# Moving a bias load and reordering the first steps of a fused attention and dense kernel on one core

## The chip, the cores and the metric

The kernel runs on one core of one Trainium2 chip. The metric is the device time of one execution in microseconds (us). A profiled execution also gives a trace; its span runs from the first to the last instruction. In the profile PE is TensorE, PEld its weight loads, DVE VectorE, ACT ScalarE, POOL GpSimd and SP the engine that issues most DMAs; ACTq and SPq are the queues on which ACT and SP issue.

## The reference

Input x is 2048 x 512 in bf16. It is normalised once, and two branches use the result:

```
xn = layernorm(x)
A: q, k, v = xn @ wqkv, in 32 heads of 16
   pq, pk = q @ w_phi, k @ w_phi            (16 x 16 per head)
   phi(p) = [softmax(p), softmax(-p)]
   kv = phi_k^T v;  z = sum of phi_k
   A = ((phi_q kv) / (phi_q z + 1e-6)) @ wo
B: h = xn @ w1 + b1                          (1792 hidden units)
   B = (h * tanh(softplus(h))) @ w2          (Mish)
out = x + A + B
```

## The kernel before

The 2048 tokens are 16 tiles of 128, in four groups of four. w_phi is folded into the key and query weights: `wT`, the key (later the query) part of wqkv, is loaded turned by a transposing DMA (line 143); `Wbd` holds w_phi as a block-diagonal matrix (line 524); the fold (line 156) multiplies the two, and its result is copied to `wkp` (line 165).

The order of the work is written by hand: the scheduler is off, and one string, `STEPS`, lists 433 steps, which line 623 issues one after the other. Each engine takes its own instructions in that order and waits only on data and buffers. `@n` behind a step is the PSUM bank it takes, one of six; a step that takes a bank waits until the bank's last reader is done. `v` or `a` behind a copy says whether DVE or ACT makes it. The steps that matter here:

- `LS i`, `RS i`, `AZ i`, `TP i`, `TC i`: for the four tiles of group 0, statistics (170, 172), inverse root on POOL (176, 177), normalisation (181), turning on PE (560), copy of the turned tile to `xnT` (565). `LN g` and `AP g k` do the same for a later group, turned by DMA (186).
- `WB`: Wbd. `F0 kt`, `FD kt`: fold and copy for the keys; `WT`, `F`, `FC` the same for the queries.
- `PB`: the bias, loaded as 14 x 128, is turned on PE (533); `CB` copies it to `b1f` (605), which every Mish reads.
- `LP`: the first two tiles' key logits (209). `L s i`, `LC`: logits of a tile (194) and their copy (252); `WL` the same in a wide bank. `V t`, `VC t`: values (194) and copy (218). `H u`, `M u`: one 128-unit piece of the hidden layer for four tiles (228) and its Mish (239).
- `E`, `X`, `S`, `R`, `N`: extremes, exponentials (288), sums (305), inversion and scaling (340) of the softmaxes; `A` accumulates kv (387); `KV` masks it; `W`, `Q`, `G`, `C` do the queries (366, 418, 433, 455).
- `O t`, `P t`, `Y t`: second layer (463), projection by wo (470), addition of x and store (477, 478). `OH`, `PH`, `YH` are the last tile in two parts.
- `DX g`, `DW i`: loads of x groups 2 and 3 and of w2 and wo, on SP.

Before the first step the kernel issues the loads of lines 483 to 493 and, on PE, `WARM` matmuls on a constant (513), which compute nothing that is used:

```
nc.sync.dma_start(x_sb[:, 0, :], x_v[:, 0, :])
wT_of = {0: load_turned(D)}
...
nc.scalar.dma_start(wsrc[:], wphi_v)
nc.scalar.dma_start(x_sb[:, 1, :], x_v[:, 1, :])
nc.scalar.dma_start(b1b[:], b1_v[:, :])
nc.sync.dma_start(x_sb[:, 2:4, :], x_v[:, 2:4, :])
nc.sync.dma_start(wv[:], wqkv_v[:, :, 2 * D : 3 * D])
nc.sync.dma_start(w1_sb[:, :, 0 : 7 * P], w1_v[:, :, 0 : 7 * P])
nc.sync.dma_start(x_sb[:, 4:8, :], x_v[:, 4:8, :])
nc.sync.dma_start(w1_sb[:, :, 7 * P : F], w1_v[:, :, 7 * P : F])
```

The line numbers in the text are those of the kernel before; in the changed kernel they are one lower in most places.

Of the kernel before, what the change touches and what calls it, by code (L numbers as in the profile page):

```python
# [19 lines left out]

WARM = 12
STEPS = """
LS 0; RS 0; DX 2; LS 1; WB; RS 1; AZ 0; TP 0 @0; F0 0 @1; F0 1 @2; AZ 1; FD 0 v; TP 1 @3; TC 1 v; LS
2; PB @4; RS 2; TC 0 a; LS 3; RS 3; FD 1 a; AZ 2; F0 2 @5; F0 3 @0; FD 2 a; FD 3 a; LP i @1,2; KM;
DX 3; AZ 3; V 0 @3; LC 0 0 a; TP 2 @5; V 1 @0; TC 2 a; TP 3 @1; VC 0 a; LC 0 1 v; TC 3 v; CB; L 0 2
@5; L 0 3 @2; LC 0 3 a; LN 1; H 0 @3; H 1 @1; H 2 @4; M 0; LC 0 2 a; H 3 @2; M 1; M 2; M 3; VC 1 a;
E 0 0; H 4 @3; H 5 @5; AP 1 0; H 6 @1; H 7 @4; M 4; H 8 @2; M 5; H 9 @0; M 6; M 7; H 10 @3; M 8; M
9; M 10; AP 1 1; H 11 @5; E 0 1; V 4 @1; X 0 1; WL 1; LN 2; V 6 @4; VC 4 a; X 0 0; L 1 0 @2; L 1 3  # L30
@0; LC 1 0 a; V 5 @3; LN 3; VC 5 a; H 12 @1; WL 2; H 13 @2; VC 6 a; S 0 0; LC 1 3 a; M 11; V 3 @3; M
12; M 13; H 14 @4; H 15 @0; H 16 @5; H 17 @1; VC 3 a; M 14; H 18 @2; M 15; M 16; M 17; LC 1 2 a; H
19 @3; AP 2 0; AP 2 1; AP 3 0; L 2 0 @4; LC 2 0 a; L 2 1 @0; LC 2 1 a; V 2 @5; S 0 1; L 2 2 @1; M
18; LC 1 1 a; M 19; H 20 @4; LC 2 2 a; AP 3 1; H 21 @0; WT; H 22 @2; M 20; VC 2 a; R 0 1 v; L 2 3
@3; H 23 @1; R 0 0 v; N 0 1; M 21; N 0 0; H 24 @4; M 22; LC 2 3 a; F 0 @5; F 1 @0; E 1 0; E 1 1; M
23; M 24; F 2 @2; E 2 0; E 2 1; FC 0 a; H 25 @3; H 26 @1; FC 1 a; H 27 @4; M 25; M 26; L 3 2 @5; FC
2 a; M 27; V 7 @0; L 3 3 @3; V 11 @1; F 3 @2; L 3 0 @4; LC 3 0 v; LC 3 2 a; L 3 1 @5; A 0 0; X 1 0;
X 1 1; A 0 1; LC 3 3 a; FC 3 v; S 1 0; V 8 @4; LC 3 1 a; VC 7 a; L 4 0 @2; E 3 0; VC 8 a; LC 4 0 a;
L 4 1 @3; LC 4 1 a; L 4 3 @5; VC 11 a; L 4 2 @0; X 2 0; V 9 @4; L 5 0 @2; H 28 @3; H 29 @1; VC 9 a;
LC 4 2 v; M 28; M 29; H 30 @0; H 31 @4; H 32 @3; M 30; H 33 @1; H 34 @0; M 31; M 32; M 33; M 34; H  # L40
35 @4; M 35; H 36 @3; M 36; S 1 1; LC 4 3 a; R 1 0 v; E 3 1; LC 5 0 a; N 1 0; R 1 1 v; H 37 @1; H 38
@0; H 39 @4; H 40 @3; H 41 @5; H 42 @2; S 2 0; A 1 0; M 37; N 1 1; M 38; M 39; M 40; A 1 1; M 41; M
42; X 3 0; L 6 3 @1; L 5 2 @0; V 10 @4; VC 10 a; L 5 1 @3; LC 5 2 a; L 6 0 @5; E 4 0; E 4 1; X 2 1;
S 3 0; V 15 @2; VC 15 a; V 13 @4; VC 13 a; LC 6 0 a; R 2 0 a; S 2 1; DW 3; R 3 0 a; X 3 1; L 6 1 @0;
LC 5 1 a; DW 2; N 3 0; N 2 0; L 5 3 @2; O 0 @4; S 3 1; V 12 @5; V 14 @3; LC 6 1 a; LC 5 3 a; O 1 @0;
L 6 2 @2; R 2 1 a; N 2 1; VC 14 a; LC 6 3 a; VC 12 v; R 3 1 a; N 3 1; X 4 0; A 2 0; S 4 0; LC 6 2 a;
A 2 1; A 3 0; W 4 0 v; X 4 1; H 43 @3; M 43; A 3 1; H 44 @1; H 45 @5; M 44; H 46 @2; M 45; H 47 @3;
M 46; M 47; H 48 @1; KV; H 49 @5; H 50 @2; Q 0 0; M 48; M 49; G 0 0; M 50; H 51 @3; H 52 @1; H 53
@5; S 4 1; W 4 1 v; M 51; M 52; H 54 @2; H 55 @3; Q 0 1; M 53; E 5 0; E 5 1; M 54; E 6 0; L 7 0 @1;
M 55; G 0 1; C 0 a; X 5 0; LC 7 0 a; L 7 1 @5; X 5 1; O 2 @2; O 3 @3; LC 7 1 a; L 7 2 @1; LC 7 2 a;  # L50
S 5 0; Q 1 0; L 7 3 @5; G 1 0; E 6 1; W 5 0 a; P 0; P 1; Y 0; Q 1 1; O 4 @1; G 1 1; LC 7 3 a; O 5
@4; S 5 1; Q 2 0; O 6 @5; C 1 a; P 2; G 2 0; W 5 1 v; Y 1; Q 2 1; P 3; O 7 @0; E 7 0; X 6 0; S 6 0;
G 2 1; Q 3 0; C 2 a; G 3 0; Y 2; Y 3; X 6 1; O 8 @2; Q 3 1; W 6 0 v; E 7 1; S 6 1; P 4; P 5; G 3 1;
C 3 a; Q 4 0; X 7 0; Y 4; W 6 1 v; X 7 1; S 7 0; O 9 @3; O 10 @1; G 4 0; Q 4 1; P 6; P 7; G 4 1; Y
5; Y 6; C 4 a; Q 5 0; W 7 0 a; G 5 0; O 11 @4; Q 5 1; Y 7; O 12 @5; S 7 1; G 5 1; C 5 a; Q 6 0; G 6
0; O 13 @0; Q 6 1; G 6 1; W 7 1 v; P 8; P 9; Q 7 0; C 6 a; G 7 0; P 10; P 11; Y 8; Q 7 1; G 7 1; O
14 @2; Y 9; Y 10; C 7 a; P 12; P 13; OH 0 @3; PH 0; Y 11; P 14; OH 1 @1; PH 1; Y 12; Y 13; YH 0; Y
14; YH 1
"""


# [1 line left out]
def kernel(  # L63
# [12 lines left out]
    nc = tc.nc  # L76
    P = 128
    S, D, NH, DH, F = 2048, 512, 32, 16, 1792
# [15 lines left out]
    b1_v = B_b1.rearrange("(f p) -> f p", p=P)  # L94
# [21 lines left out]
    b1b = wts.tile([FT, P], BF16, name="b1b")  # L116
# [29 lines left out]
    def bank(b, name, dtype=FP32):  # L146

        return ps.tile([P, 512], dtype, name=name, tag=f"bank{b}")
# [336 lines left out]
    with nc.allow_non_contiguous_dma(reason="tiny w_phi load"):  # L485
        nc.scalar.dma_start(wsrc[:], wphi_v)
    nc.scalar.dma_start(x_sb[:, 1, :], x_v[:, 1, :])
    nc.scalar.dma_start(b1b[:], b1_v[:, :])
    nc.sync.dma_start(x_sb[:, 2:4, :], x_v[:, 2:4, :])
    nc.sync.dma_start(wv[:], wqkv_v[:, :, 2 * D : 3 * D])  # L490
    nc.sync.dma_start(w1_sb[:, :, 0 : 7 * P], w1_v[:, :, 0 : 7 * P])
    nc.sync.dma_start(x_sb[:, 4:8, :], x_v[:, 4:8, :])
    nc.sync.dma_start(w1_sb[:, :, 7 * P : F], w1_v[:, :, 7 * P : F])

# [16 lines left out]
    warm = bank(5, "warm")  # L511
    for _ in range(WARM):
        nc.tensor.matmul(
# [142 lines left out]
```

## Time and profile before

| | us |
|---|---|
| median of 3 runs (lowest, highest) | 173.84 (173.68, 174.01) |
| the profiled execution, its own time | 174.0 |
| its span | 172.3 |
| ACT busy on Mish, 56 times | 37.2 |
| DVE busy on sums, 16 times | 36.4 |
| DVE idle for x from memory, 3 times | 4.3 |
| wv from issue to landing | 4.5 |

Busy time is what an engine spent in its instructions; matmuls overlap one another, so a busy PE does not say how closely they follow. For that the chain of work that ended last is read: it goes back from the last instruction, at each step to what released it or to the instruction ahead of it on its engine, and lists pieces as start, length and what. In the timeline a line is start, length, engine, source line, operation, output<-input and count, with the idle time ahead of it and its cause in brackets. In an answer on one source line the three durations are the least, the median and the greatest.

### The profile page before, as it was taken

The page shows a single profiled execution, that of the slowest core. Times are in us where ns is not written, and L with a number is a line of the kernel's source. Part 1 is how long each engine was busy: PE and PEld are TensorE (multiplying, and loading weights), DVE is VectorE, ACT ScalarE, POOL GpSimd, SP SyncE. Part 2 cuts the span into 40 slices and gives each one's busy share as a digit, 9 for nine tenths or more (in the row PEclk, how much of TensorE's full clock was granted, in tenths as well). Part 3 has the DMA queues.
Part 4 walks back from the last instruction along what each step waited for, and adds up shares of the span by engine and source line. Part 5 has one row for each costly group of instructions (what it writes and reads, how often), then busy time and mean ns, then how long its engine had stood idle before and what let it go on. Part 6 is the DMA issues. An engine that isn't in the chain of part 4 may idle for free.

```text
span 172.3 us, 2713 instructions
## 1 busy us (share of the span) xinstructions
PE 168.7 (98%) x1039; PEld 82.4 (48%) x1039; DVE 143.2 (83%) x221; ACT 119.5 (69%) x192; POOL 9.4 (5%) x26
## 2 busy tenths in 40 slices
PE   8999999999999999999999999999999999999993
PEld 2554444444545444454446544444444545445452
DVE  2878998999997999979999999799988996844433
ACT  2446889979899998989999988974063883414200
POOL 4332205000000000000000000000000000000000
PEclk9999999999999999999999999999999999999999
DMA  5999350199930000000000363023974749885641
GB/s 98 269 377 365 82 98 0 37 189 207 366 120 0 0 4 0 0 0 0 4 0 0 64 118 66 12 51 67 150 152 93 150 95 144 172 168 100 173 134 61
DMA packets 44953, 18.02 MB, mean 105 GB/s; under 512 B 37004, under 2 KB 44940, under 8 KB 44940
## 3 DMA queue, kind: packets, MB, share of 16 engines
q1 hardware_dynamic: 44096, 17.60, 44.5%
q10 hardware_dynamic: 844, 0.25, 0.6%
q8 instruction: 8, 0.13, 0.3%
q14 instruction: 5, 0.04, 0.1%
HBM read 6.84 MB, written 2.10 MB: 52 GB/s over the span
## 4 chain that ended last, share of the span: by engine, by line
PE 95%; DMA 3%; SPq 0%; DVE 0%; issue 0%
PE po L463 28%; PE ph L228 28%; PE pl L194 14%; PE po L470 8%; PE pv L194 8%; DMA wT<-in_A_wqkv_dram 3%; PE pnd L418 2%; PE pkv L387 2%; PE pfold L156 1%; PE pwide L194 1%; PE pl L209 1%; PE ptr L560 0%; SPq L483 0%; DVE x_sb L477 0%; PE pb L533 0%
## 5 line engine op out<-in xcount | busy, mean ns | idle before, releaser
L463 PE MATMUL po<-w_sb,acts 128*128 128x512 bf16 (+2 forms) x238 | 50.7, 366 | 0.0
L228 PE MATMUL ph<-xnT,w_sb 128*128 128x512 bf16 x224 | 50.1, 379 | 0.0
L239 ACT ACTIVATE acts<-ph,b1f 128x512 bf16<-128x512 f32 x56 | 37.2, 694 | 4.6 <-PE ph L228 4.4
L305 DVE TENSOR_REDUCE s<-e 128x128 f32<-128x2048 bf16 x16 | 36.4, 2279 | 2.5 <-ACT e L288 2.5
L228 PEld LDWEIGHTS <-w_sb 128*128 128x128 bf16 x224 | 21.7, 98 | 25.5
L463 PEld LDWEIGHTS <-acts 128*128 128x128 bf16 x238 | 22.3, 98 | 24.1
L288 ACT ACTIVATE e<-e 128x2048 bf16<-128x2048 bf16 x16 | 30.3, 1908 | 0.0
L194 PEld LDWEIGHTS <-xnT 128*128 128x128 bf16 x184 | 17.6, 98 | 20.1 <-DMA wv<-in_A_wqkv_dram 0.2
L252 ACT CAST p_sb<-pl 128x512 bf16<-128x512 f32 x27 | 15.4, 587 | 5.5 <-PE pl L194 4.7
L433 ACT COPY ds<-pnd 128x32 f32<-128x32 f32 x16 | 2.9, 183 | 23.5 <-PE pnd L418 23.5
L194 PE MATMUL pv<-wv,xnT 128*128 128x512 bf16 x64 | 16.1, 379 | 0.0
L477 DVE TENSOR_TENSOR x_sb<-po,x_sb 128x512 bf16<-128x512 f32 (+2 forms) x17 | 10.9, 654 | 5.7 <-PE po L470 5.7
L470 PE MATMUL po<-wqk,xnT 128*128 128x512 bf16 (+2 forms) x68 | 15.5, 366 | 0.0
L194 PE MATMUL pl<-wqk,xnT 128*128 128x512 bf16 x64 | 15.3, 379 | 0.0
L170 DVE BATCH_NORM_STATS2 stats<-x_sb 128x6 f32<-128x512 bf16 x16 | 10.1, 679 | 4.3 <-DMA x_sb<-in_A_x_dram 4.3
L263 DVE TENSOR_TENSOR m<-m 128x512 bf16<-128x512 bf16 (+1 forms) x32 | 11.5, 358 | 1.1
L194 PE MATMUL pl<-wkp,xnT 128*128 128x512 bf16 x48 | 11.7, 379 | 0.0
L263 DVE TENSOR_TENSOR m<-p_sb 128x1024 bf16<-128x1024 bf16 x16 | 10.9, 682 | 0.2 <-ACT p_sb L252 0.2
L272 DVE TENSOR_TENSOR e<-p_sb,m 128x2048 bf16<-128x2048 bf16 x8 | 9.8, 1226 | 1.4 <-PE pkv L387 1.1
L272 DVE TENSOR_TENSOR e<-m,p_sb 128x2048 bf16<-128x2048 bf16 x8 | 9.8, 1225 | 0.3
L340 DVE TENSOR_TENSOR e<-e,r 128x2048 bf16<-128x2048 bf16 x8 | 9.6, 1215 | 0.0
L138 ACT ACT_TABLE_LOAD x7 | 9.0, 1283 | 0.1
(62 smaller groups left out, 131.4 us busy)
## 6 DMA issues: line engine op xcount, KB each, us to landing
out_dram<-x_sb SPq DMA_DIRECT2D x15, 128.0 KB, 2.0
w_sb<-in_B_w_dram SPq DMA_DIRECT2D x2, 896.0 KB, 7.8
x_sb<-in_A_x_dram SPq DMA_DIRECT2D x3, 512.0 KB, 10.0
w_sb<-in_B_w_dram SPq DMA_DIRECT2D x2, 640.0 KB, 8.8
wv<-in_A_wqkv_dram SPq DMA_DIRECT2D x1, 512.0 KB, 4.5
wqk<-in_A_wo_dram SPq DMA_DIRECT2D x1, 512.0 KB, 4.6
w_sb<-in_B_w_dram SPq DMA_DIRECT2D x1, 512.0 KB, 9.6
x_sb<-in_A_x_dram SPq DMA_DIRECT2D x1, 256.0 KB, 3.2
```

The costliest lines, as they stand in the source:

```text
L170: nc.vector.bn_stats(stats[:, i, :], xs[:, i, :])
L194: nc.tensor.matmul(pp, lhsT=xnT[:, t, kt, :], rhs=w[:, kt, :], start=(kt == 0), stop=(kt == KT - 1),)
L228: nc.tensor.matmul(ph_of[u][:], lhsT=w1_sb[:, kt, f * P : (f + 1) * P], rhs=xnT[:, g * TPG : (g + 1) * TPG, kt, :], start=(kt == 0), stop= ...
L239: nc.scalar.activation(acts[:, f, g * 512 : (g + 1) * 512], ph_of.pop(u)[:], ACT.Mish, bias=b1f[:, f : f + 1])
L252: copy(p_of[s][:, i, :], pl_of.pop((s, i)))
L263: nc.vector.tensor_tensor(out=m[:], in0=src[:, :, 0:half], in1=src[:, :, half : 2 * half], op=op)
L272: nc.vector.tensor_tensor(out=e_of[s][:].rearrange("p t j l c -> p (t j) l c")[:, :, pl, :].rearrange("p t (c e o) -> p t c e o", e=8, o=2 ...
L288: nc.scalar.activation(v, v, ACT.Exp)
L305: nc.vector.reduce_sum(t[:], pair(s, k).rearrange("p t j l (c e) -> p (t j l c) e", e=16), axis=AX.X)
L463: nc.tensor.matmul(po_of[t, c.stop][:, c], lhsT=acts[:, f, t * P : (t + 1) * P], rhs=w2_sb[:, f, c], start=(f == 0), stop=False,)
L470: nc.tensor.matmul(po_of[t, c.stop][:, c], lhsT=oT_of[t // 2][:, t % 2 * 4 + j, :], rhs=wo_sb[:, j, c], start=False, stop=(j == 3),)
L477: nc.vector.tensor_tensor(out=y, in0=po_of.pop((t, c.stop))[:, c], in1=y, op=ALU.add)
```

## The change

- The bias is loaded on SP's queue behind the first half of w1, no longer on ACT's queue behind x's second tile.
- Eleven warm-up matmuls in place of twelve.
- The whole step list has a new order. In the head `AZ 0` and `TP 0` come ahead of `WB`; `PB` moves from among the folds to behind `L 0 3`; `H 0` comes ahead of `L 0 3`; `CB` comes behind `LN 1` on DVE; `LN 2` follows at once, ahead of `E 0 0`. Further on, steps of all kinds change places and banks, and some copies change engine: `VC` on ACT 15 to 11, `LC` on ACT 29 to 30, `R` on ACT 4 to 6, `C` on ACT 8 to 7, the rest of each on DVE.

The steps themselves and their functions are unchanged. The diff, with the step list cut after its head:

```
-WARM = 12
+WARM = 11
 STEPS = """
-LS 0; RS 0; DX 2; LS 1; WB; RS 1; AZ 0; TP 0 @0; F0 0 @1; F0 1 @2; AZ 1; FD 0 v; TP 1 @3; TC 1 v; LS
-2; PB @4; RS 2; TC 0 a; LS 3; RS 3; FD 1 a; AZ 2; F0 2 @5; F0 3 @0; FD 2 a; FD 3 a; LP i @1,2; KM;
-DX 3; AZ 3; V 0 @3; LC 0 0 a; TP 2 @5; V 1 @0; TC 2 a; TP 3 @1; VC 0 a; LC 0 1 v; TC 3 v; CB; L 0 2
-@5; L 0 3 @2; LC 0 3 a; LN 1; H 0 @3; H 1 @1; H 2 @4; M 0; LC 0 2 a; H 3 @2; M 1; M 2; M 3; VC 1 a;
-E 0 0; H 4 @3; H 5 @5; AP 1 0; H 6 @1; H 7 @4; M 4; H 8 @2; M 5; H 9 @0; M 6; M 7; H 10 @3; M 8; M
...
+LS 0; RS 0; LS 1; AZ 0; TP 0 @0; TC 0 a; WB; RS 1; F0 0 @1; F0 1 @2; AZ 1; FD 1 a; TP 1 @3; FD 0 v;
+F0 2 @4; F0 3 @5; TC 1 v; FD 2 a; FD 3 a; LP i @0,1; LC 0 0 a; DX 2; LS 2; LC 0 1 a; RS 2; LS 3; DX
+3; V 0 @2; RS 3; AZ 2; TP 2 @3; TC 2 a; V 1 @4; AZ 3; KM; TP 3 @5; L 0 2 @0; TC 3 v; LC 0 2 a; H 0
+@1; L 0 3 @3; VC 1 a; PB @5; LC 0 3 a; H 1 @0; H 2 @4; H 3 @3; LN 1; CB; LN 2; AP 1 0; AP 1 1; M 0;
+E 0 0; M 1; AP 2 0; E 0 1; M 2; M 3; LN 3; H 4 @1; M 4; V 3 @0; VC 3 a; VC 0 a; H 5 @5; H 6 @4; M 5;
...
+LC 3 1 a; V 5 @2; L 4 0 @1; E 2 1; VC 6 v; V 2 @5; L 4 3 @3; VC 2 a; LC 4 0 a; X 1 1; N 0 0; V 9 @4;
...
 """
@@
-    nc.scalar.dma_start(b1b[:], b1_v[:, :])
     nc.sync.dma_start(x_sb[:, 2:4, :], x_v[:, 2:4, :])
     nc.sync.dma_start(wv[:], wqkv_v[:, :, 2 * D : 3 * D])
     nc.sync.dma_start(w1_sb[:, :, 0 : 7 * P], w1_v[:, :, 0 : 7 * P])
+    nc.sync.dma_start(b1b[:], b1_v[:, :])
     nc.sync.dma_start(x_sb[:, 4:8, :], x_v[:, 4:8, :])
     nc.sync.dma_start(w1_sb[:, :, 7 * P : F], w1_v[:, :, 7 * P : F])
```

More of the change, by code (lines that the diff above doesn't have):

```diff
@@ L30 @@
[L30 to L58, printed above, removed]
+LS 0; RS 0; LS 1; AZ 0; TP 0 @0; TC 0 a; WB; RS 1; F0 0 @1; F0 1 @2; AZ 1; FD 1 a; TP 1 @3; FD 0 v;
+F0 2 @4; F0 3 @5; TC 1 v; FD 2 a; FD 3 a; LP i @0,1; LC 0 0 a; DX 2; LS 2; LC 0 1 a; RS 2; LS 3; DX
@@ new lines @@
+3; V 0 @2; RS 3; AZ 2; TP 2 @3; TC 2 a; V 1 @4; AZ 3; KM; TP 3 @5; L 0 2 @0; TC 3 v; LC 0 2 a; H 0
+@1; L 0 3 @3; VC 1 a; PB @5; LC 0 3 a; H 1 @0; H 2 @4; H 3 @3; LN 1; CB; LN 2; AP 1 0; AP 1 1; M 0;
+E 0 0; M 1; AP 2 0; E 0 1; M 2; M 3; LN 3; H 4 @1; M 4; V 3 @0; VC 3 a; VC 0 a; H 5 @5; H 6 @4; M 5;
+M 6; H 7 @3; M 7; H 8 @1; H 9 @0; M 8; H 10 @2; H 11 @5; H 12 @4; M 9; M 10; M 11; H 13 @3; WL 1; H
+14 @1; H 15 @0; L 2 0 @2; M 12; H 16 @5; M 13; X 0 0; LC 2 0 a; AP 2 1; X 0 1; L 1 0 @4; LC 1 0 v; S
@@ new lines @@
+0 0; L 1 3 @3; LC 1 3 a; H 17 @2; M 14; H 18 @4; V 4 @3; WL 2; M 15; M 16; M 17; M 18; AP 3 0; AP 3
+1; L 2 1 @1; H 19 @0; LC 1 2 a; M 19; H 20 @5; L 2 2 @2; LC 1 1 a; M 20; L 2 3 @4; H 21 @0; LC 2 3
+a; M 21; LC 2 2 a; H 22 @5; H 23 @4; H 24 @0; M 22; M 23; WT; F 0 @2; LC 2 1 a; FC 0 a; VC 4 v; H 25
+@3; R 0 0 v; H 26 @5; M 24; S 0 1; H 27 @4; F 1 @1; E 1 0; M 25; M 26; E 1 1; F 2 @2; F 3 @0; M 27;
+FC 3 a; FC 1 a; E 2 0; R 0 1 a; V 6 @3; V 7 @5; VC 7 a; X 1 0; L 3 0 @4; LC 3 0 a; L 3 1 @0; FC 2 v;
@@ new lines @@
+LC 3 1 a; V 5 @2; L 4 0 @1; E 2 1; VC 6 v; V 2 @5; L 4 3 @3; VC 2 a; LC 4 0 a; X 1 1; N 0 0; V 9 @4;
+S 1 0; VC 5 v; V 10 @0; L 4 2 @5; R 1 0 a; N 0 1; A 0 0; VC 9 v; V 8 @1; VC 8 v; LC 4 3 a; X 2 1; L
+3 3 @2; LC 3 3 v; X 2 0; S 1 1; L 3 2 @3; N 1 0; L 4 1 @4; LC 4 1 a; A 0 1; V 11 @1; VC 11 a; S 2 0;
+R 2 0 v; R 1 1 a; VC 10 a; LC 4 2 a; H 28 @2; H 29 @4; H 30 @1; N 1 1; LC 3 2 a; E 3 0; M 28; S 2 1;
+A 1 0; E 3 1; H 31 @0; H 32 @5; H 33 @3; H 34 @2; M 29; M 30; M 31; M 32; M 33; H 35 @4; H 36 @1; H
@@ new lines @@
+37 @0; H 38 @5; H 39 @3; M 34; M 35; N 2 0; DW 3; M 36; M 37; M 38; M 39; H 40 @2; H 41 @4; H 42 @1;
+M 40; M 41; H 43 @0; M 42; M 43; H 44 @5; M 44; H 45 @3; L 5 2 @2; A 1 1; A 2 0; L 5 3 @4; L 5 0 @1;
+H 46 @0; M 45; L 5 1 @5; X 3 1; LC 5 0 a; LC 5 3 a; E 4 0; E 4 1; LC 5 1 a; S 3 1; V 14 @3; V 12 @1;
+X 3 0; DW 2; VC 12 a; V 15 @4; S 3 0; O 0 @5; X 4 0; VC 14 a; V 13 @1; LC 5 2 a; L 6 0 @3; VC 15 a;
+L 6 2 @2; R 3 0 a; R 2 1 a; O 1 @4; S 4 0; R 3 1 a; LC 6 0 a; LC 6 2 a; VC 13 a; N 3 0; N 2 1; L 6 3
@@ new lines @@
+@3; H 47 @2; H 48 @1; N 3 1; A 2 1; W 4 0 v; A 3 0; A 3 1; E 5 0; X 4 1; KV; M 46; E 5 1; LC 6 3 a;
+M 47; M 48; H 49 @0; M 49; H 50 @3; H 51 @2; M 50; M 51; L 6 1 @1; S 4 1; H 52 @0; Q 0 0; G 0 0; M
+52; H 53 @3; LC 6 1 a; M 53; H 54 @2; Q 0 1; G 0 1; H 55 @0; M 54; L 7 0 @1; L 7 3 @3; E 6 0; M 55;
+W 4 1 v; L 7 2 @2; LC 7 0 a; O 2 @0; C 0 a; LC 7 3 a; X 5 0; O 3 @1; L 7 1 @3; LC 7 2 a; Q 1 0; X 5
+1; G 1 0; E 6 1; S 5 0; W 5 0 v; LC 7 1 a; O 4 @2; Q 1 1; G 1 1; P 0; S 5 1; C 1 a; O 5 @3; Y 0; X 6
@@ new lines @@
+0; Q 2 0; P 1; W 5 1 v; E 7 0; G 2 0; Y 1; O 6 @5; S 6 0; Q 2 1; P 2; P 3; Y 2; G 2 1; C 2 a; Q 3 0;
+G 3 0; W 6 0 a; O 7 @4; Q 3 1; G 3 1; O 8 @0; P 4; P 5; E 7 1; Q 4 0; X 6 1; Y 3; C 3 a; O 9 @1; Y
+4; X 7 0; S 6 1; G 4 0; Q 4 1; G 4 1; W 6 1 v; S 7 0; O 10 @2; P 6; Y 5; Y 6; W 7 0 v; P 7; C 4 a; Y
+7; X 7 1; S 7 1; Q 5 0; G 5 0; O 11 @3; Q 5 1; O 12 @5; G 5 1; Q 6 0; C 5 a; O 13 @4; W 7 1 a; G 6
+0; Q 6 1; P 8; G 6 1; P 9; Y 8; C 6 v; Q 7 0; P 10; P 11; G 7 0; Q 7 1; Y 9; Y 10; O 14 @0; OH 0 @1;
@@ L59 @@
+G 7 1; C 7 a; P 12; P 13; PH 0; P 14; OH 1 @2; Y 11; PH 1; Y 12; Y 13; YH 0; Y 14; YH 1
 """
```

## The prediction

> **What bounds the kernel now.** I read the page's engine shares first, then the chain of work that ended last, in order of time.
>
> ```profile
> PE 168.7 (98%) x1039; PEld 82.4 (48%) x1039; DVE 143.2 (83%) x221; ACT 119.5 (69%) x192; POOL 9.4 (5%) x26
> ```
>
> ```profile
> 1.25 5.36 DMA wT<-in_A_wqkv_dram
> 6.61 0.05 issue
> 6.65 0.62 PE pfold L156 x8
> ...
> 8.16 1.73 PE pl L209 x8
> ...
> 13.78 10.36 PE ph L228 x48
> ...
> 169.41 0.24 PE po L470 x4
> 169.65 0.02 issue
> 169.67 0.29 DVE x_sb L477
> ```
>
> From the first fold at 6.65 to the last projection at 169.65 every piece of the chain is TensorE, and 48 hidden-layer matmuls take 10.36, 0.216 us each, which is also the pace of any other stretch of that chain. So TensorE streams for 163.0 us without a gap. Profiled time = 6.65 (until wT has landed) + 163.0 + 2.6 (172.3 - 169.65, last addition and store) + 1.7 (174.0 against the span) = 174.0. The median of the runs is 173.84, 0.16 below this execution; I take off the same 0.16 at the end.
>
> The change has the same matmuls after the warm-ups. So it can win only ahead of 6.65 or behind 169.65, and it can lose wherever the new order opens a gap in 163 us of TensorE. The other views are for these two questions: the timeline of the first 25 us, and the line that loads wT.
>
> ```profile
> 1.25 3.12 SPq L143 DMA_TRANSPOSE wT<-in_A_wqkv_dram  x1
> ...
> 1.83 0.67 ACTq L488 DMA_DIRECT2D b1b<-in_B_b_dram  x1
> ...
> 5.24 0.41 DVE L524 TENSOR_TENSOR Wbd<-block,wsrc 128x512 bf16<-128x512 bf16 x1
> ...
> 5.57 0.41 DVE L181 TENSOR_SCALAR xn<-x_sb,mv,rstd 128x512 bf16<-128x512 bf16 x1
> ...
> 6.03 0.53 PE L560 MATMUL ptr<-ident,xn 128*128 128x128 bf16 x4
> ...
> 13.43 2.47 DVE L170 BATCH_NORM_STATS2 stats<-x_sb 128x6 f32<-128x512 bf16 x4 [0.83 <-DMA x_sb<-in_A_x_dram]
> ...
> 14.69 0.69 ACT L239 ACTIVATE acts<-ph,b1f 128x512 bf16<-128x512 f32 x1 [0.28 <-PE ph L228]
> ...
> 15.82 0.36 DVE L172 BATCH_NORM_AGGREGATE mv<-stats 128x2 f32<-128x6 f32 x4
> ```
>
> ```profile
> L143 SPq DMA_TRANSPOSE wT<-in_A_wqkv_dram x2: 1819/2470/3120, 1.2 to 38.0; - x2
> ...
> DMA to landing us min/median/max: 5.0/5.2/5.4
> ```
>
> **Part 1: first tile ahead of the weights by block, eleven warm-ups.** The normalisation (0.41) takes the place of Wbd at 5.24 and ends at 5.65; Wbd follows at 5.57 to 5.98. TP 0 starts 0.05 behind its input, as now (5.98 to 6.03): 5.70 instead of 6.03. The eleventh warm-up starts at 5.04 and streams 0.43, so PE is free at 5.47 (with twelve it would be 5.90, 0.2 late). TP 0 is through at about 6.17. By itself this is worth nothing: the fold waits for wT until 6.61 either way. Its worth is that the fold could now start at 6.17, where before TP 0 held PE until 6.56; so an earlier wT pays up to 0.48, not 0.09.
>
> **Part 2: the bias leaves ACT's queue.** Does wT land earlier? Its issue takes 3.12 at 1.25, while ACT issues x's second tile (0.52 at 1.28) and the bias (0.67 at 1.83); the second wT load, at 38.04 with no ACT load beside it, takes 1.82 to issue and 5.0 to land, not 5.36. Bounds: nothing (the bias is 3.5 KB) and the whole 0.36; a loss I exclude, since nothing is put ahead of wT. I charge the 0.36 by issue time to the two ACT loads inside it: 0.67/1.19 x 0.36 = 0.20, my value. The x, wv and w1 loads stand behind wT on the same queue and move with it.
>
> The Trainium skill (DMA: Bandwidth & Descriptors, "Issuing engines are not separate DMA queues") says that loads issued on several engines run on the same 16 DMA engines and interleave, and that spreading them saves only issue time. By that the bias's few packets cost wT nothing and the sum has 0 here. The 3.12 against 1.82 speaks against it, but two executions of one line with other traffic are no proof.
>
> **Part 3: bias behind w1.** SP issues one load more (0.67 by ACT's row) ahead of x tiles 4 to 7, w1's second half and x 8 to 15. The queue is not empty then: DMA moves 269, 377 and 365 GB/s in slices 2 to 4 (4.3 to 17.2), so a later issue is hidden, and 3.5 KB at that rate is 0.01. It would cost up to 0.67 if the cover were gone. The bias itself lands behind w1's first half (issued 5.54, landed 6.4 later, 11.94) and its turn PB stands at 14.4 on PE: 2 us spare.
>
> **Part 4: the new head on PE**, laid out by the rows' durations (0.863 for four 512-wide matmuls, 0.22 for four 128-wide), wT as before. PB (0.06 to 0.11) leaves the folds. The first logits would start 0.11 earlier, but their second matmul needs xnT of tile 1, copied by DVE at 7.69 to 8.10: 8.14 instead of 8.21, 0.07 won, which PB takes back later. From there V 0 9.66, TP 2, V 1, TP 3, L 0 2 at 11.82, H 0 12.69 (w1 landed 11.94; TC 3 done 12.45), L 0 3, PB 14.41, H 1 14.47, H 2, H 3, **H 4 17.07**.
>
> H 4 is where it is tight. It takes H 0's bank, free after M 0, and M 0 now needs CB, which stands on DVE behind LN 1's four statistics. These wait for x 4 to 7 (13.43) and end at 16.10; CB 0.16, M 0 16.30 to 16.99, so H 4 can start at 17.04. Spare: 0.03. Before, M 0 ran at 14.69 and CB at 12.44. Behind CB, DVE waits in LN 2 for x 8 to 11 (issued 7.36, landed 10.0 later: 17.4); AP 1, E 0 0, AP 2 0 and E 0 1 queue behind it and end at about 27.9. X 0 0 wants them at 28.8 (M 13 and a table load first) and L 2 0 wants tile 8 turned at 29.2 (AP 2 0 24.9, landed 3.3 later: 28.3). Both hold.
>
> **Part 5: the rest of the order.** I set ACT's and DVE's new orders against PE's gapless times with paces from the timeline (one half of the extremes 2.98, one sum 2.20, a copy 0.60 on DVE and 0.47 to 0.58 on ACT, a Mish 0.68). The least spare is at L 4 3, PE 53.36: it takes V 6's bank, which VC 6, now on DVE, frees. From L 1 0's end (31.94) DVE has LC 1 0, S 0 0, AP 3, VC 4, R 0 0, S 0 1, E 1 0, E 1 1, E 2 0, FC 2, E 2 1, VC 6: 0.60 + 2.20 + 1.30 + 0.60 + 1.19 + 2.20 + 3 x 2.98 + 0.60 + 2.97 + 0.68 = 21.28, to 53.22. Spare 0.1. Elsewhere 0.3 or more (H 34 behind M 28: 0.3; Q 2 0 behind W 5 0: 1 to 2). Four value copies and one combine go from ACT to DVE, one key copy and two inversions the other way; neither engine is the bound (83% and 69%). At the tail the same PE work stands in nearly the same order (OH 0 ahead of P 12), Q 7 1 ends at 159.95 and PH 0 starts at 167.0 as now, so C 7 and its turn keep their 7 us, and the last addition and store stay: no change.
>
> **Sum.** -0.20 (wT) +- 0.1 for tight places at 0.03 and 0.1 spare: 174.0 - 0.2 = 173.8 against this execution, 173.65 against the median.
>
> **Rivals.**
> - *The bias never cost anything, or the gain is given back at H 4.* If wT stays at 6.61, or x 4 to 7 stay at 13.43 while PE is 0.2 early, H 4 waits and all is as before: 173.8. For it: the bias is tiny, the spare 0.03. Against: the issue times.
> - *The whole 0.36 to 0.48 is won* (wT at 6.2): 173.4. For it: Part 1 just clears the way. Against: x's second tile is still issued beside wT.
> - *Slower: CB behind LN 1.* Place: M 0, then H 4. Once x 4 to 7 land later than 13.46, PE stands idle one for one; with SP's extra 0.67 not hidden, H 4 starts 0.64 late: 174.5. It is slower by 0.2% from a landing at 13.8 on. Against: full DMA rate.
> - *Slower: a slow TensorE clock past the folds.* The warm-ups are 0.43 apart against 0.216 later, though the granted clock reads 1.00 throughout; full pace first shows at TP 0's end and the folds (6.2 to 6.65). Warm-ups now end 0.43 sooner, with an idle of up to 0.45 ahead of the fold. If the switch then comes late, each us at half pace costs 0.5; at worst as long again as the first slow stretch (5.4 us): +2.7. The Trainium skill (TensorE: Matmul & The Clock Gate, Part 1) has a window of some 3.4 us judged as a whole; by it the next chance comes 3.4 us on, an estimate of +1.6. For the sum I take 0: from 0.83 to 6.17 PE would idle only from 5.47 to 5.70.
>
> **Chances.** Forecast 0.40 (0.08 of it beyond 0.2%), whole gain 0.14, nothing or given back 0.18, CB 0.14, clock 0.07, a spare misjudged (0.4 to 0.8 lost) 0.07. About 0.2% (0.35 us) is what a measurement of this kernel tells from no change. Faster 0.22, same 0.50, slower 0.28. Range: 173.35 (whole gain) to 174.6 (CB); beyond it lie the clock and stray misses.
>
> **What would show it.** wT's issue well under 3.12 and the first fold near 6.4; TP 0 at 5.70; M 0 right behind CB near 16.1 and no idle before H 4; PE gapless from fold to end, still 163.0. Wrong if wT's issue stays at 3.1, if PE idles at H 4 or L 4 3, or if the folds run at 0.11 a matmul.

## The result and the profile after

| | before | after |
|---|---|---|
| median of the runs compared, us | 173.92 | 174.6 |
| lowest to highest | 173.68 to 174.22 | 174.44 to 175.01 |
| ratio (95% interval) | | 1.0043 (1.0029 to 1.0057) |
| profiled execution, its own time / span | 174.0 / 172.3 | 174.48 / 172.8 |
| first fold starts | 6.65 | 6.50 |
| last projection starts | 169.41 | 169.91 |

The changed kernel is 0.7 us slower. The forecast was 173.65, with 0.50 on no change that can be measured. Here and below a ratio compares only the executions within 1.5% of a kernel's fastest, which leaves out three of twelve of wt_az, one of six of wt_r2_cb and three of six of cb_late.

The engine shares come first, from the page of the changed kernel:

```profile
PE 168.3 (97%) x1038; PEld 82.2 (48%) x1038; DVE 143.5 (83%) x222; ACT 118.1 (68%) x191; POOL 9.1 (5%) x26
```

TensorE is still the bound, at 97% of its span instead of 98%. The chain of work that ended last shows where time was lost. The columns are start, length and what; issue is time in which nothing that the profile shows was waited for:

```profile
1.25 5.20 DMA wT<-in_A_wqkv_dram
6.45 0.05 issue
6.50 0.62 PE pfold L155 x8
...
7.79 1.91 PE pl L208 x8
...
97.34 1.28 ACT L137
98.62 0.01 issue
98.63 0.70 ACT acts L238
99.33 0.04 issue
99.37 2.75 PE ph L227 x12
...
169.91 0.24 PE po L469 x4
170.15 0.02 issue
170.17 0.29 DVE x_sb L476
```

The fold starts 0.15 sooner, yet the last projection starts 0.50 later. So 0.65 was lost in between, 163.41 us of TensorE instead of 162.76. In the chain of before every piece in this stretch was TensorE. Here the chain leaves TensorE: from 83.74 to 99.37 it runs through ScalarE and VectorE, and comes back at a hidden-layer piece (ph) that waited for a Mish (acts). The timeline of these microseconds shows why; brackets hold the idle time ahead of an instruction and what ended it:

```profile
89.75 0.35 ACT L321 ACTIVATE log<-s 128x128 f32<-128x128 f32 x1
...
90.13 2.29 DVE L304 TENSOR_REDUCE s<-e 128x128 f32<-128x2048 bf16 x1 [1.66 <-ACT log L321]
...
92.34 3.49 DVE L339 TENSOR_TENSOR e<-e,r 128x2048 bf16<-128x2048 bf16 x3
93.65 0.42 ACT L313 ACTIVATE r<-log 128x256 bf16<-128x256 f32 x1 [2.25 <-DVE e L339]
...
98.63 0.69 ACT L238 ACTIVATE acts<-ph,b1f 128x512 bf16<-128x512 f32 x1
...
99.37 0.81 PE L227 MATMUL ph<-xnT,w_sb 128*128 128x512 bf16 x3 [0.31 <-ACT acts L238]
```

Read it with the new order `R 3 0 a; R 2 1 a; O 1; S 4 0; R 3 1 a; ...; N 3 0; N 2 1` and the buffer counts of the code: `s`, the sums, has three, `r2`, the inverted sums, has two. `S 4 0` is the fourth sum in flight, so VectorE stands 1.66 until `R 3 0`'s logarithm on ScalarE has read its sum and so freed a buffer. `N 3 0` stands behind `S 4 0` on VectorE and starts only at 92.34. `R 3 1` is the third inversion in flight: its exponential on ScalarE needs the buffer that `N 3 0` frees, and ScalarE stands 2.25. Behind it on ScalarE are the copies, `X 4 1`, a table load and `M 46`, which frees the bank that `H 49` takes. The order before finished `N 3 0` and `N 2 1` ahead of `R 3 1`, and `N 3 1` ahead of `S 4 0`.

The head, from the timeline of its first 20 us:

```profile
1.25 2.81 SPq L142 DMA_TRANSPOSE wT<-in_A_wqkv_dram  x1
...
5.02 0.41 DVE L180 TENSOR_SCALAR xn<-x_sb,mv,rstd 128x512 bf16<-128x512 bf16 x1
...
5.49 0.40 PE L559 MATMUL ptr<-ident,xn 128*128 128x128 bf16 x4
...
13.25 2.47 DVE L169 BATCH_NORM_STATS2 stats<-x_sb 128x6 f32<-128x512 bf16 x4 [0.92 <-DMA x_sb<-in_A_x_dram]
...
13.43 1.03 PE L193 MATMUL pl<-wkp,xnT 128*128 128x512 bf16 x4
...
14.39 0.18 PE L532 MATMUL pb<-ident,b1b 14*128 14x14 bf16 x1
...
14.50 3.63 PE L227 MATMUL ph<-xnT,w_sb 128*128 128x512 bf16 x16
...
15.92 0.14 DVE L604 CAST b1f<-pb 128x14 f32<-128x14 bf16 x1
...
16.09 3.00 ACT L238 ACTIVATE acts<-ph,b1f 128x512 bf16<-128x512 f32 x5 [1.01 <-DVE b1f L604]
```

`TP 0` is at 5.49, so the first tile is out of the fold's way. The issue of wT takes 2.81 instead of 3.12. `CB` (15.92) stands behind `LN 1` (13.25) as foreseen, and `M 0` runs at 16.09, in this execution just in time for `H 4`. `PB` (14.39) now stands between `L 0 3` and `H 1`: the four matmuls of `L 0 3` start at 13.43 and at the pace of 0.216 each would be followed at 14.29, but `H 1` starts at 14.50, 0.21 later. In the timeline of before `H 0` follows the logits at once:

```profile
13.62 10.52 PE L228 MATMUL ph<-xnT,w_sb 128*128 128x512 bf16 x48
```

Counted by the starts of matmuls, TensorE needs 7.14 from the first fold to `H 1` without the 0.86 of `H 0` (14.50 - 6.50 - 0.86), and before it needed 6.97 to `H 0` (13.62 - 6.65). So 0.17 of the 0.65 is lost in the head, and the buffers account for nearly all the rest.

### The profile page after: what moved, and what is told of

The parts are those of the page before. It is cut to its first block, busy times and chain, and to the rows that moved or that the text cites. A ratio compares the mean times of both kernels' runs of the same rounds, so it can differ in the third digit from the quotient of the medians.

```text
span 172.8 us, 2706 instructions
## 1 busy us (share of the span) xinstructions
PE 168.3 (97%) x1038; PEld 82.2 (48%) x1038; DVE 143.5 (83%) x222; ACT 118.1 (68%) x191; POOL 9.1 (5%) x26
## 4 chain that ended last, share of the span: by engine, by line
PE 86%; ACT 7%; DMA 3%; DVE 2%; SPq 0%; issue 0%; ACTq 0%
PE ph L227 27%; PE po L462 25%; PE pl L193 12%; PE po L469 8%; PE pv L193 6%; ACT e L287 3%; DMA wT<-in_A_wqkv_dram 3%; PE pnd L417 2%; PE pkv L386 1%; DVE s L304 1%; ACT p_sb L251 1%; PE pfold L155 1%; ACT vext L217 1%; PE pl L208 1%; PE pwide L193 1%; ACT L137 1%
## 5 line engine op out<-in xcount | busy, mean ns | idle before, releaser
L227 PE MATMUL ph<-xnT,w_sb 128*128 128x512 bf16 x224 | 51.1, 379 | 0.3 <-ACT acts L238 0.3
L238 ACT ACTIVATE acts<-ph,b1f 128x512 bf16<-128x512 f32 x56 | 36.2, 701 | 4.0 <-PE ph L227 2.7
L193 PEld LDWEIGHTS <-xnT 128*128 128x128 bf16 x184 | 17.6, 98 | 20.3
L251 ACT CAST p_sb<-pl 128x512 bf16<-128x512 f32 x28 | 15.9, 588 | 4.0 <-PE pl L193 3.2
L193 PE MATMUL pl<-wqk,xnT 128*128 128x512 bf16 x64 | 15.8, 379 | 0.0
L469 PEld LDWEIGHTS <-xnT 128*128 128x128 bf16 x68 | 6.2, 98 | 6.0
```

The source lines that it names most:

```text
L193: nc.tensor.matmul(pp, lhsT=xnT[:, t, kt, :], rhs=w[:, kt, :], start=(kt == 0), stop=(kt == KT - 1),)
L227: nc.tensor.matmul(ph_of[u][:], lhsT=w1_sb[:, kt, f * P : (f + 1) * P], rhs=xnT[:, g * TPG : (g + 1) * TPG, kt, :], start=(kt == 0), stop= ...
L238: nc.scalar.activation(acts[:, f, g * 512 : (g + 1) * 512], ph_of.pop(u)[:], ACT.Mish, bias=b1f[:, f : f + 1])
L251: copy(p_of[s][:, i, :], pl_of.pop((s, i)))
L469: nc.tensor.matmul(po_of[t, c.stop][:, c], lhsT=oT_of[t // 2][:, t % 2 * 4 + j, :], rhs=wo_sb[:, j, c], start=False, stop=(j == 3),)
```

## The experiments

The theory at this point, A: the loss is the two waits for buffers at `R 3 1`, and what is left comes from the head, above all `H 4` waiting for `M 0` behind `CB` behind `LN 1`. Rivals: the loss lies in the head alone; or the bias's new queue costs it. Three measures serve throughout: the ratio to the kernel before, run on the same chip; the start of the first fold; and the stream, the time from the first fold to the start of the last projection (162.76 before, 163.41 after). Fold and stream are of one profiled execution each.

**More buffers.** Two kernels differ from the changed one in one number each.

```
r2_three:  r2 = r_of[s, k] = smx.tile([P, 128, 2], BF16, name="r2", bufs=3)     # was 2
s_four:    t = s_of[s, k] = smx.tile([P, 128], FP32, name="s", bufs=4)          # was 3
```

Expected of the first: 

> The changed kernel with three buffers for r2 in place of two. Theory A (a wait on buffers: R 3 1 on ACT waits for r2 until N 3 0, N 3 0 stands on DVE behind S 4 0, and S 4 0 waits for a buffer of s that ACT frees late; 2.25 us on ACT make M 46 and so H 49 late): the 2.25 us wait of L313 is gone, M 46 starts near 96.4, PE has no idle time at H 49, the span falls by 0.4 to 0.5 and the ratio to the kernel before to 1.000 to 1.002. Theory B (ACT has too much to do before M 46, or the lost time lies elsewhere): M 46 stays within 0.5 of 98.6 or the idle time of PE comes up at a later place, ratio still 1.004.

Expected of the second: 

> The changed kernel with four buffers for s in place of three, r2 still two. Theory A: S 4 0 starts at about 88.4 instead of 90.13, N 3 0 can follow R 3 0 at 90.6, R 3 1 waits 0.3 to 0.5 instead of 2.25, M 46 is early enough for H 49: ratio 1.000 to 1.002, as with three r2. If only r2 counts (A without the first half of the chain): R 3 1 still waits over 2, ratio 1.004. Theory B: 1.004.

Measured: 1.0017 (1.0004 to 1.0029) and 1.0020 (1.0008 to 1.0031). The stream of r2_three is 162.94, 0.47 less than the changed kernel's. Its timeline:

```profile
90.42 2.29 DVE L304 TENSOR_REDUCE s<-e 128x128 f32<-128x2048 bf16 x1 [1.66 <-ACT log L321]
...
91.72 0.42 ACT L313 ACTIVATE r<-log 128x256 bf16<-128x256 f32 x1
...
96.70 0.69 ACT L238 ACTIVATE acts<-ph,b1f 128x512 bf16<-128x512 f32 x1
```

VectorE still waits 1.66 for a buffer of `s`, and that costs nothing. What is gone is the idle time ahead of the exponential, and `M 46` ends 2 us sooner. In s_four it is VectorE's wait that is gone, ScalarE's is 0.59, and the ratio is the same. Either remedy breaks the pair of waits; it takes both to lose time.

**The same by the order alone.** In the changed kernel one step moves; the buffers are as they were.

```
-O 1 @4; S 4 0; R 3 1 a; LC 6 0 a; LC 6 2 a; VC 13 a; N 3 0; N 2 1;
+O 1 @4; N 3 0; S 4 0; R 3 1 a; LC 6 0 a; LC 6 2 a; VC 13 a; N 2 1;
```

Expected: 

> The changed kernel with one step moved: N 3 0 ahead of S 4 0 on VectorE; buffers as they are. Theory A (S 4 0 waits on VectorE for a buffer of s that R 3 0's logarithm on ScalarE frees, N 3 0 stands behind it, and R 3 1's power on ScalarE waits for the buffer of r that N 3 0 frees): N 3 0 now runs while S 4 0's buffer is awaited, the power no longer waits 2.2 us, H 49 has no idle; like three buffers of r: 1.0017 (1.0005 to 1.0030). If it is not the place in VectorE's queue but the count of buffers or something else about that stretch: 1.0043 as the changed kernel.

Measured: 1.0012 (1.0002 to 1.0022), stream 162.94. Its timeline:

```profile
90.86 1.23 DVE L339 TENSOR_TENSOR e<-e,r 128x2048 bf16<-128x2048 bf16 x1 [2.11 <-ACT r L313]
...
92.00 2.28 DVE L304 TENSOR_REDUCE s<-e 128x128 f32<-128x2048 bf16 x1
92.18 0.42 ACT L313 ACTIVATE r<-log 128x256 bf16<-128x256 f32 x1 [0.50 <-DVE e L339]
...
97.17 0.69 ACT L238 ACTIVATE acts<-ph,b1f 128x512 bf16<-128x512 f32 x1
```

With `N 3 0` ahead in VectorE's queue, ScalarE waits 0.50 instead of 2.25 and `H 49` does not wait. Three remedies, by two buffers and one place, give 1.0012 to 1.0020: the pair of waits is worth 0.0023 to 0.0031 of the time, 0.40 to 0.54 us. Each of these ratios is uncertain by some 0.0012, and the intervals of the two buffer runs just touch the changed kernel's; that the idle time at `H 49` is gone in all three profiles, and 0.47 of the stream in two of them, is the firmer evidence.

**A control.** The kernel before with the third buffer of `r2`. Expected: 

> Control: the kernel before with three buffers of r instead of two. Theory A: the order before has no such wait, 1.0000 (0.9993 to 1.0007). Rival: a third buffer of r is worth something in any order, then what it gave the changed kernel (0.26%) says nothing of the change: 0.998. Its profile is a second look at the head of the order before: if landings vary between executions, the fold starts elsewhere than 6.65, between 6.3 and 6.9.

Measured: 0.9996 (0.9986 to 1.0006). The buffer is worth nothing where the order does not need it. Its profile gives a second look at the head before: fold at 6.61, wT's issue 2.92.

**The bias back on ScalarE's queue**, in the changed kernel.

```
+    nc.scalar.dma_start(b1b[:], b1_v[:, :])          # behind x tile 1, as before
-    nc.sync.dma_start(b1b[:], b1_v[:, :])            # behind the first half of w1
```

Expected: 

> The changed kernel with the bias on ACT's queue again, behind x's second tile. If the bias slows the load of wT: issue of wT back from 2.81 to about 3.1, landing from 5.20 to about 5.36, first fold at 6.65, and 0.1 to 0.2 us slower than the changed kernel, ratio 1.005. If it costs nothing: fold at 6.50 +- 0.05, ratio 1.004 as the changed kernel.

Measured: 1.0047 (1.0032 to 1.0062), with fold 6.46 and wT's issue 3.09. This cannot be told from the changed kernel's 1.0043. The 0.20 us that the prediction charged is 0.0012 and would be hidden in these intervals, so the ratio does not settle it; the landings of wT, further down, show no difference by the queue.

**The head alone, in the order before.** head_only has `AZ 0` and `TP 0` ahead of `WB`, eleven warm-ups, the bias behind w1, `PB` behind `L 0 2`; head_late is the same with `PB` behind `L 0 3`; az_only has the bias and `PB` as before.

```
-LS 0; RS 0; DX 2; LS 1; WB; RS 1; AZ 0; TP 0 @0; F0 0 @1;
+LS 0; RS 0; DX 2; LS 1; AZ 0; TP 0 @0; WB; RS 1; F0 0 @1;
-WARM = 12
+WARM = 11
head_only:  L 0 2 @5; PB @4; CB; L 0 3 @2;
head_late:  L 0 2 @5; L 0 3 @2; PB @4; CB;
```

Expected: 

> The kernel before with the head's parts alone: bias behind w1's first half, AZ 0 and TP 0 ahead of WB, eleven warm-ups, PB and CB behind L 0 2; every other step in the old order. If the head is what it seemed in the trace of the changed kernel (fold 0.15 sooner, PB 0.1 dearer where it stands now): ratio 0.998 to 1.000, span 172.1 to 172.3, PE gapless after the first logits. Rival (the head itself loses, by a late clock or PB's place): 1.001 or more, with idle time or slow matmuls before 20 us.

Expected: 

> The order before with only the head's parts: first tile normalised ahead of the weights by block, eleven warm-ups, bias behind w1 on SyncE's queue, and PB behind L 0 3 (in head_only it stood behind L 0 2 and PE waited for the bias to land at 12.42, which took back 0.39 of a fold that started at 6.11). Theory A (a sooner fold is worth its time where nothing downstream takes it back): PB does not wait, from the fold to the last projection's start 162.8 to 163.0, ratio 0.9990 (0.9980 to 1.0000). Theory B (the head wins nothing; the start of the fold varies from execution to execution by wT's landing and the second tile's, as much in the order before): ratio 1.0005 to 1.0010, PB's 0.1 to 0.2 lost.

Expected: 

> The kernel before with only the first tile normalised ahead of the weights by block and eleven warm-ups; the bias stays on ACT's queue and its turn PB in the head. If the bias on ACT's queue holds wT back by 0.2 us, as the prediction charged: wT's issue near 3.1, fold near 6.6, ratio 1.0000. If the queue makes no difference (the spread of wT's issue, 2.77 to 3.26 in the profiles so far, is that of executions): as early a fold as with the bias behind w1, no PB in the stretch, ratio 0.9985 to 0.9995, at or below head_late's.

Measured: 1.0007 (0.9996 to 1.0018), 1.0012 (1.0004 to 1.0021) and 1.0005 (0.9996 to 1.0014). None is faster, though their folds start at 6.11, 6.17 and 6.24. In head_only TensorE waited for the bias, which landed at 12.42 (stream 163.15); moving `PB` back took that wait away and did not show in the ratio. head_late needs 7.14 from the first fold to `H 0` (13.31 - 6.17), the same 0.17 more than before as the changed kernel. In az_only nothing takes the sooner fold back (stream 162.81), and yet the ratio is not below 1. Its timeline shows the issue of wT short with the bias beside it:

```profile
1.25 2.77 SPq L143 DMA_TRANSPOSE wT<-in_A_wqkv_dram  x1
...
1.83 0.67 ACTq L488 DMA_DIRECT2D b1b<-in_B_b_dram  x1
...
6.24 0.66 PE L156 MATMUL pfold<-Wbd,wT 128*128 128x128 bf16 x8
```

What this profile shows is one lucky execution: at 173.62 it is the lowest of its eleven runs, 0.28 below their median, while the profile of before, at 174.0, lay 0.08 above its median of 173.92. The start of the first fold in every profile in which wT's issue was not moved:

| first tile | bias's queue | fold starts, one per kernel |
|---|---|---|
| behind Wbd | ScalarE's | 6.61, 6.65 |
| ahead of Wbd | ScalarE's | 6.24, 6.24, 6.46 |
| ahead of Wbd | SyncE's | 6.11, 6.17, 6.31, 6.36, 6.42, 6.50, 6.65, 6.75, 6.78, 6.79 |

The last row spans 0.68 under one treatment, so the 0.15 between the two profiles of before and after tells nothing. The landing of wT does not sort by the queue either: 4.9 to 5.4 after its start with the bias on ScalarE's queue (five kernels, mean 5.1), 4.8 to 5.5 on SyncE's (ten kernels, mean 5.2).

**CB ahead of LN 1**, with three buffers of `r2` (r2_cb) and alone (cb_first).

```
-H 3 @3; LN 1; CB; LN 2;
+H 3 @3; CB; LN 1; LN 2;
```

Expected of r2_cb: 

> The changed kernel with three buffers of r instead of two, and the bias's copy CB ahead of LN 1's statistics on VectorE. Theory A (the loss is the two waits on buffers at R 3 1, about 0.45 us; the bias's turn PB inside the gapless stretch, about 0.2; and H 4 waiting for M 0 behind CB behind LN 1, 0 to 0.4 by how late x tiles 4 to 7 land): CB runs near 14.6 to 15.0, M 0 before 16, H 4 without idle whenever the tiles land; from the first fold to the last projection's start 162.9 to 163.0 us as with three buffers alone (162.94); ratio 1.0005 (1.0000 to 1.0010). Theory B (what three buffers leave, 0.17%, is the new head itself and not CB): the ratio stays at 1.0017.

Expected of cb_first: 

> The changed kernel with CB ahead of LN 1 and nothing else. Theory A: the waits at R 3 1 stay, ACT stands 2.2 us ahead of the power and H 49 starts 0.45 late, but H 4 never waits: ratio 1.003 (1.0025 to 1.0035), between the changed kernel's 1.0043 and 1.0017 with three buffers. Theory B: CB is worth nothing, 1.0043.

Measured: 1.0008 (1.0000 to 1.0017) and 1.0040 (1.0027 to 1.0052). Beside 1.0017 and 1.0043 without the edit, both go the right way and neither interval tells it apart. The profiles are clearer. Of five kernels that have `CB` behind `LN 1`, the 16 matmuls of `H 1` to `H 4` take 3.63 in three, as they should, and 3.89 and 3.93 in the two where x tiles 4 to 7 landed latest (s_four, bias_back). The chain of s_four runs through them:

```profile
14.13 2.47 DVE stats L169 x4
16.60 0.28 DVE mv L171 x4
16.88 0.07 DVE b1f L604
...
16.97 0.70 ACT acts L238
...
17.71 1.02 PE ph L227 x4
```

Tiles landed at 14.11 cost 0.26 here; in r2_three, where their statistics start at 13.40, they cost nothing. The mean over the five is 0.11.

r2_cb shows another wall. Its fold is early, at 6.31, and then `V 0` waits for wv:

```profile
10.07 1.04 PE L193 MATMUL pv<-wv,xnT 128*128 128x512 bf16 x4 [0.56 <-DMA wv<-in_A_wqkv_dram]
```

**CB still later**, behind `LN 2`, with three buffers of `r2`, to price the wait.

```
-H 3 @3; LN 1; CB; LN 2;
+H 3 @3; LN 1; LN 2; CB;
```

Expected: 

> The changed kernel with three buffers of r and CB put still later on VectorE, behind LN 2 instead of LN 1. Theory A (TensorE stands idle at H 4 one for one with the wait CB, M 0): CB near 20.2 (LN 2's statistics wait for x tiles 8 to 11, 17.3, and end at 20.1), M 0 20.3 to 21.0, H 4 at 21.0 instead of 17.4, 3.6 us lost: ratio 1.022 (1.018 to 1.025). Theory B (M 0 or H 4 is not on the path): 1.0017 as with CB behind LN 1.

Measured: 1.0288 (1.024 to 1.0336), more than the 1.022 expected; executions from 177.48 to 181.15, the profiled one 180.66. TensorE waited 3.84 at `H 4`, as expected. The rest is in the busy time by stretch. The columns are the stretch, its length, busy time and instructions of TensorE, its weight loads, VectorE, ScalarE and POOL, the granted TensorE clock, DMA share and GB/s:

```profile
17.30:21.10 3.80, 0.00 (x0) 0.00 (x0) 3.58 (x12) 0.74 (x2) 1.15 (x3) 0.81 0.09 27
21.10:25.00 3.90, 3.90 (x10) 1.43 (x10) 3.76 (x9) 2.66 (x5) 0.77 (x1) 0.50 0.90 90
25.00:30.00 5.00, 5.00 (x22) 2.07 (x20) 4.86 (x10) 3.56 (x7) 0.00 (x0) 0.85 0.62 92
```

The granted clock fell to 0.50 while TensorE stood idle and stayed there to about 26.5. From 21.1 on that is 5.4 us at half pace, 2.7 lost; 3.84 + 2.7 = 6.5, and 180.66 is 6.5 above the median of r2_three (174.17). The lowest execution, 177.48 with the full clock, is 3.3 above it. The six executions sort by their mean granted clock: 177.48 at 1.00, 179.18 and 180.00 at 0.99, 180.66 to 181.15 at 0.98. So the path is real and costs about one for one, and this idle costs a second time through the clock. The Trainium skill (TensorE: Matmul & The Clock Gate, Part 1) has the clock halved after an idle window of some 3.4 us whose phase is free. The halving and its variation between executions agree with it, and the 6.8 us at 0.50 are two such windows; but the clock fell 2.4 us into this idle (at 19.65, the last matmul ending at 17.26), before a whole window of idle had passed, and there the measurement decides.

**Sooner loads.** Two kernels issue wv ahead of x tiles 2 and 3 (az_wv from az_only, r2_cb_wv from r2_cb); three issue wT first on SyncE's queue and x tile 0 first on ScalarE's, ahead of x tile 1 and w_phi (wt_before, wt_az and wt_r2_cb, from before, az_only and r2_cb).

```
az_wv, r2_cb_wv:
+    nc.sync.dma_start(wv[:], wqkv_v[:, :, 2 * D : 3 * D])
     nc.sync.dma_start(x_sb[:, 2:4, :], x_v[:, 2:4, :])
-    nc.sync.dma_start(wv[:], wqkv_v[:, :, 2 * D : 3 * D])
wt_before, wt_az, wt_r2_cb:
-    nc.sync.dma_start(x_sb[:, 0, :], x_v[:, 0, :])
     wT_of = {0: load_turned(D)}
+    nc.scalar.dma_start(x_sb[:, 0, :], x_v[:, 0, :])
+    nc.scalar.dma_start(x_sb[:, 1, :], x_v[:, 1, :])
     nc.scalar.dma_start(wsrc[:], wphi_v)
-    nc.scalar.dma_start(x_sb[:, 1, :], x_v[:, 1, :])
```

Expected, in the order az_wv, r2_cb_wv, wt_before, wt_az, wt_r2_cb:

> The first tile normalised ahead of the weights by block and eleven warm-ups in the order before, and in addition wv issued ahead of x tiles 2 and 3 on SyncE's queue. Theory C (a sooner fold wins nothing because V 0 then waits for wv, which lands 9.0 to 10.0 and is next behind wT): wv lands some 0.5 sooner, V 0 follows the logits without a wait; ratio 0.9990 (0.9980 to 1.0000) against 1.0005 without it. Theory D (the fold itself, at the landing of wT, is no sooner in the median, whatever stands behind it): 1.0005 again. If x tiles 2 and 3 now come late, TP 2 waits and it is slower, 1.0010 or more.

> The changed kernel with three buffers of r, CB ahead of LN 1, and wv issued ahead of x tiles 2 and 3. Its run without the last edit gave 1.0008 and waited 0.56 for wv at V 0 in its profile. Theory C: no wait at V 0, ratio 0.9995 (0.9985 to 1.0005). Theory D: 1.0008 again.

> The kernel before with wT issued first on SyncE's queue (at 0.79 instead of 1.25) and x tile 0 on ScalarE's queue ahead of x tile 1 and the projection's phi weights. wT lands some 0.46 sooner, near 6.1. Theory P (the prediction's Part 1: in the order before, TP 0 starts behind Wbd and the normalisation and holds TensorE until 6.5, so a sooner wT pays little): the fold starts near 6.55, ratio 0.9993 (0.9985 to 1.0000). Theory Q (what holds the fold moves with the loads; the order of Wbd and the first tile does not matter): the fold near 6.2, ratio 0.9975.

> The same sooner wT with the first tile normalised ahead of the weights by block and eleven warm-ups. Theory P: now the order pays, the fold starts near 6.0 (Wbd through at 5.9), ratio 0.9975 (0.9965 to 0.9990) unless V 0 then waits for wv, which gives back up to 0.4: 0.9995. Theory Q: as the run without the new order of the first tile, whichever that gives.

> The changed kernel with three buffers of r, CB ahead of LN 1 and the sooner wT: what the change would be without its losses and with the gain that the prediction charged. If the head is worth its time there: 0.9990 (0.9980 to 1.0000) against 1.0008 without the sooner wT. If something else of the new head takes it (the second logits matmul waits for tile 1, whose load is where it was): 1.0000 to 1.0010.

Measured: 1.0085 (1.0068 to 1.0101), 1.0082 (1.0067 to 1.0096), 1.0123 (1.0088 to 1.0159), 1.0063 (1.0032 to 1.0093) and 1.0138 (1.0098 to 1.0177). All five are slower, and none decides between its theories: each moved another load into the way. In az_wv, x tiles 2 and 3 landed at 9.54 and their statistics waited:

```profile
9.57 0.69 DVE L170 BATCH_NORM_STATS2 stats<-x_sb 128x6 f32<-128x512 bf16 x1 [1.87 <-DMA x_sb<-in_A_x_dram]
```

In wt_before, wT's issue fell to 1.41, but x tile 1 and w_phi, both issued while it ran, came late:

```profile
0.79 1.41 SPq L143 DMA_TRANSPOSE wT<-in_A_wqkv_dram  x1
...
1.68 0.53 ACTq L487 DMA_DIRECT2D wsrc<-in_A_w_phi_dram  x1
...
5.05 0.69 DVE L170 BATCH_NORM_STATS2 stats<-x_sb 128x6 f32<-128x512 bf16 x1 [1.02 <-DMA x_sb<-in_A_x_dram]
...
6.68 0.42 DVE L524 TENSOR_TENSOR Wbd<-block,wsrc 128x512 bf16<-128x512 bf16 x1 [0.72 <-DMA wsrc<-in_A_w_phi_dram]
...
7.49 0.40 PE L560 MATMUL ptr<-ident,xn 128*128 128x128 bf16 x4 [1.85 <-DVE xn L181]
```

The shorter issue did not bring wT sooner by as much: from its start at 0.79 it took 5.5 to land in wt_before, 6.4 in wt_az and 6.2 in wt_r2_cb, so it landed at 6.3, 7.2 and 7.0, against 6.61 in the kernel before. The idle time of TensorE in these three also cost clock in some executions: in wt_az the seven at a mean clock of 1.00 took 174.03 to 175.28, the five at 0.99 took 176.41 to 177.64.

Whether the order of the first tile pays once wT lands sooner therefore stays open. No kernel tried is measurably faster than the one before.

## Why the prediction was wrong

- **What bounds the kernel: right.** TensorE still sets the time, and the loss lies in gaps of its stream, which is where the prediction said a loss could come from.
- **Part 5 failed, at "Elsewhere 0.3 or more".** The walk through the new order followed PSUM banks and the engines' queues; it did not follow the buffers of `s` (three) and `r2` (two). With them, `M 46` ends at 99.33 and `H 49` is late. This is the loss of 0.47 in the stream, and 0.40 to 0.54 by the three remedies. The rival "a spare misjudged (0.4 to 0.8 lost)" named the size, with a chance of 0.07, but not the place. The place that the walk called tightest, `L 4 3` with 0.1, held: TensorE did not wait there.
- **Part 2 failed: nothing shows that the 0.20 was the bias's.** wT's issue took 2.49 (az_wv) to 3.12 (before) with the bias on ScalarE's queue and 2.60 to 3.26 with it on SyncE's, wherever wT itself was left in place; neither the landing of wT nor the fold sorts by the queue. Nor does the landing follow the issue time: an issue of 1.41 landed after 5.5 and 6.4, one of 3.12 after 5.4. The charge by issue time made a cause out of two executions. The Trainium skill (DMA: Bandwidth & Descriptors, "Issuing engines are not separate DMA queues") was the rule weighed against it, and these runs agree with the rule.
- **Part 1 was right that the place of `TP 0` is worth nothing alone**: it started at 5.49, and az_only gives 1.0005. That it opens 0.48 for a sooner wT was not shown; by the row that the prediction shows (0.53 from 5.70) `TP 0` would have been through at 6.23, not 6.17.
- **Part 3 was right as far as it could be seen.** The later issue on SyncE is hidden: x tiles 4 to 7 landed at 13.22 after and at 13.90 in bias_back, where that queue has no bias. That landing varies by itself. The cover of `PB` was thinner than the 2 us only where `PB` was put earlier (head_only).
- **Part 4 was right about the places and mis-sized `PB`.** The second matmul of the first logits waits for tile 1: `V 0` starts 1.85 behind them instead of 1.72, so 0.13 is lost. That `PB` is gone from the folds wins 0.17 (the first logits start 1.18 behind the fold instead of 1.35). Between `L 0 3` and `H 1`, `PB` then costs 0.21, not the 0.06 to 0.11 that the prediction gave it. Together 0.17 is lost, where the prediction had 0.07 won and taken back. `H 4` with its spare of 0.03 is the rival "CB behind LN 1"; it is true in two of five profiles, at 0.26 and 0.30, and shown at about one for one by cb_late. It is a part of the loss, 0.11 in the mean, and not the 0.7 that its place in the range stood for.
- **The clock rival did not happen.** The granted clock is 1.00 throughout the head after, and eight fold matmuls take 0.62 as before. cb_late shows that the mechanism exists at a longer idle.
- **The sum.** In the profiled executions: -0.15 (fold) + 0.17 (head) + 0.47 (buffers) + 0.01 = 0.50 at the last projection, as measured (169.91 against 169.41). In the medians the fold's share is not there and `H 4` adds its mean: 0.17 + 0.47 + 0.11 = 0.75, an estimate, against 0.68. With the pair of waits undone by either buffer, 1.0017 and 1.0020 remain, 0.3 us; 0.17 and 0.11 fit that in size, but they are read from single executions, and no ratio measured here separates them.

## What to carry to other kernels

An order written by hand is checked against every pool that has fewer buffers than the order has values in flight, not only against banks and queues: count, at each allocation, how many of that name are still unread, and on which engine's queue the reader stands. Two waits that were harmless alone, one on each of two engines, became a stall here because the release of each stood in the other's queue; either a buffer or a swap of two steps undid it. And a difference between two profiles at a DMA's issue or landing is worth nothing until the same loads have been looked at in several executions.

## What the runs showed of the hardware that was not expected

- The first load of wT lands 4.8 to 5.5 us after its start at 1.25, in kernels that issue the same ahead of it; its issue on SyncE takes 2.49 to 3.26. Issued first, its issue took 1.40 to 1.41, yet it landed only after 5.5 to 6.4, and small loads issued beside it on ScalarE's queue landed late (w_phi 4.90 after its issue at 1.68; in the profile after the same load took 2.5).
- An idle of TensorE can cost twice. After waits of 2.28 (wt_az) and 2.69 (wt_r2_cb) the clock was granted at 0.50 for 3.4 us, after 3.84 (cb_late) for 6.8. In wt_az the halving came 1.4 us after TensorE had resumed. After 1.85 (wt_before's profile) the clock stayed at 1.00, but three of that kernel's six executions show a mean of 0.99, and seven of the twelve of wt_az kept 1.00: which idle halves the clock differs between executions, and no limit was measured.
